# Turned score tiles spilled in woven pairs, with new chunk sizes

## The chip, the cores and the metric

The kernel runs on one core of one Trainium2 chip. The metric is the device time of one execution in microseconds (us). A core has a matrix engine (PE, whose weight loads are PEld), a vector engine (DVE), a scalar engine (ACT), GpSimd (POOL), and SyncE (SP), on whose queue this kernel issues all its DMAs. Each engine works through its own list of instructions in order and waits on semaphores for the others. Sixteen DMA engines carry out what SP issues.

## The reference, cut to what matters

```python
# B=2, S=3136, D=256, d_qk=64, d_ff=1024; everything float32
scores = z @ z.T / S
out    = u * ((np.maximum(scores, 0) ** 2) @ v)          # attention, gated by u
h      = np.maximum(out @ w_in, 0)                       # first MLP
gate   = sigmoid(depthwise_conv3_along_S(h, conv_w))
x      = (h * gate) @ w_out
xn     = (x - mean(x)) / sqrt(var(x) + 1e-6) * g_ln      # second MLP, with layer norm
y      = x + np.maximum(xn @ w_ch1, 0) @ w_ch2
```

## The kernel before, in words

The matrix engine works at reduced precision, so every operand is split in a high part and a remainder, and a product takes three matmuls (high·high, remainder·high, high·remainder).

Attention goes over the queries in chunks. `TILES` gives the chunk sizes of one batch in tiles of 128 tokens (the last tile is half full; 24.5 tiles are one batch); with two batches there are 14 chunks. For chunk `c` and each key tile `j` of 25, two matmuls make the scores in `s` (128 keys x up to 512 queries), ACT takes relu (`a<-s`) and square (`a<-a`; in the first two chunks DVE multiplies a part of them instead), a copy rounds to the high part (`ah<-a`, mostly on ACT), DVE makes the remainder (`al<-a,ah`), and six matmuls add `v` times these into `av`. When a chunk is through, DVE multiplies `av` by `u` (`u<-av,u`), and the result goes to DRAM as `gated`.

The scores are symmetric. So a chunk computes only the key tiles of itself and of later chunks, and those of later chunks are kept: DVE turns each in blocks of 32x32 (`bl<-a`, STREAM_TRANSPOSE), and `spill` writes it to a DRAM tensor `turned`, with four DMAs a tile (one for each band of 32 partitions). A later chunk loads such a tile instead of computing it (`land<-turned`), and goes on with `ah<-land` and `al<-land,ah`. The turned tiles live in four buffers of the tag `bl`, each one tile wide; a buffer is free again when the last DMA out of it has landed. Tiles `a` and `land` share six buffers.

The two MLPs run in 17 blocks of three tiles (the last two of two), each released when its chunks are through: `hps` (first up-projection), the convolution in `t`, `gh` and `gl`, `y` (down-projection), the layer norm, `tps`, `h2ps`, `g2h`, `g2l`, `y`. The last three blocks take their `h` buffers for odd steps from `bl`. Early in the program DVE, ACT and POOL also decode the four weight matrices (`wn`, `wc` and `wih`, `wil` and so on).

The order on each engine is not written by hand. The program is a list of operations with prices, engines and due times (`Program`); a planner walks through it in planned time and lets each engine take the due operation whose inputs and buffers are free. Its plan fixes the order on all five queues. Where it sees a gap on PE, it puts filler matmuls on a tile of zeros (`warm_ps<-zero`, later `y<-zero` or `av<-zero`), which keep PE occupied:

```python
n = int((gaps.get(o, 0.0) - 0.1) / FILL)      # FILL = 0.125 us
```

`LAG0` sets how far behind the attention the first MLP blocks are due. In the planner a spill of `w` columns takes 1.92 us of SP, and lands after 1.9 us plus `w`/300.

Of the kernel before, what the change touches and what calls it, by code (L numbers as in the profile page):

```python
# [8 lines left out]
F32 = mybir.dt.float32  # L9
F32R = mybir.dt.float32r  # L10
U32 = mybir.dt.uint32
AF = mybir.ActivationFunctionType
ALU = mybir.AluOpType
PSUM = bass.MemoryType.PSUM

P = 128
NB, S, D, DQ, DFF = 2, 3136, 256, 64, 1024
# [2 lines left out]
NJ = S // P + 1  # L20
ZW = NJ * P
EPS = 1e-6
TILES = [4, 4, 3, 4, 3, 3, 4]
SQ = 32
PAIR = False
MIRROR = 0
SIZES = [3] * 15 + [2, 2]
WARM = 20
FILL = 0.125
LAG0 = 120.0  # L30
LAG1 = 6.0
LAG2 = 10

# [34 lines left out]
}  # L68

AFTER = {"PE": 0.2, "ACT": 0.165, "DVE": 0.15, "POOL": 0.13, "SP": 0.0}  # L70
RATE, LANDS = 300.0, 1.9
ENGINES = ("PE", "ACT", "DVE", "POOL", "SP")

# [16 lines left out]
class Program:  # L90
# [7 lines left out]
    def op(self, ways, fn, reads=(), writes=(), adds=(), takes=(), due=None, late=None, name="", port=False, kb=None):  # L98


        o = Op()
        o.ways, o.fn, o.due, o.late, o.name, o.port, o.kb = ways, fn, due, late, name, port, kb
        o.before, o.after, o.n = set(), [], len(self.ops)
        o.adds, o.spare = tuple(adds), None
        for k in reads:
            assert k in self.writers, (name, k)
            o.before.update(self.writers[k])
            self.readers.setdefault(k, []).append(o)
        for k in writes:
            o.before.update(self.writers.get(k, ()))  # L110
            o.before.update(self.readers.pop(k, ()))
            self.writers[k] = [o]
        for k in adds:
            o.before.update(self.readers.get(k, ()))
            self.writers.setdefault(k, []).append(o)
        o.before.discard(o)
        bufs = []
        for k in (*reads, *writes, *adds, *((t,) for t in takes)):
            if isinstance(k[0], Buf) and k[0] not in bufs:
                bufs.append(k[0])  # L120
        for b in bufs:
            b.users.append(o)
        o.bufs = bufs
        self.ops.append(o)
        return o

    @staticmethod
    def lasts(o, engine=None, us=None):
        if engine is None:
            engine, us = o.ways[0]  # L130
        return us + (o.late if o.late is not None else AFTER[engine])

# [139 lines left out]
def plan():  # L272
# [5 lines left out]
    for b in range(NB):  # L278
        for i in range(len(TILES)):
            q1 = min(b * S + sum(TILES[: i + 1]) * P, (b + 1) * S)  # L280
            chunks.append((q0, q1))
# [12 lines left out]
def attn_moe_kernel(ctx: ExitStack, tc: tile.TileContext, zt, ut, v, w_in, conv_w, w_out, g_ln, w1, w2, out):  # L294
    nc = tc.nc
    chunks, blocks, after = plan()
    NC, NK = len(chunks), len(blocks)
    CW = max(b - a for a, b in chunks)
# [5 lines left out]
    pool = ctx.enter_context(tc.tile_pool(name="work", bufs=1))  # L304
# [7 lines left out]
    hl = const.tile([P, ZW], F32R, name="hl")  # L312
# [10 lines left out]
    def maker(tag, places, where, shape, dtype):  # L323
# [7 lines left out]
        for tag, places, where, shape, dtype in (  # L331
            ("zst", 1, pool, [P, 512], F32),
            ("st", 2, pool, [P, 1024], F32),
            ("bl", 4, pool, [P, CW], F32),
            ("wc", 1, pool, [P, 512], U32),
            ("wn", 1, pool, [P, 512], U32),
            ("cst", 1, pool, [P, 3 * NF, 2], U32),
# [31 lines left out]
    op = pr.op  # L369
    orders = {}  # L370

    def buf(tag, fixed=False, kind=None):
        if fixed:
            orders[tag] = orders.get(tag, 0) + 1
        return Buf(tag, orders[tag] if fixed else None, kind)

    def at(b, name=None):

        if b.ap is None:
            b.ap = tags[b.tag][1](name or b.tag)  # L380
        return b.ap
# [3 lines left out]
    def price(kind, n):  # L385
        return PRICE[kind](n)
# [16 lines left out]
    def dma(fn, kb, **kw):  # L403
        return op([("SP", 0.45)], lambda e: fn(), late=LANDS + kb / RATE, kb=kb, **kw)
# [5 lines left out]
    def hl_keys(o, n):  # L410
        return [("hl", i, x) for i, (a, b) in enumerate(zp) if a < o + n and o < b for x in "hl"]
# [181 lines left out]
    def half(t, n, a=0, e=None, name=None):  # L593

        return at(t, name)[:, : 2 * n].rearrange("p (k t) -> p k t", k=2)[:, :, a : n if e is None else e]
# [3 lines left out]

    per = len(TILES)  # L600
    start_of = [sum(TILES[:i]) for i in range(per + 1)]
    chunk_of = [i for i, n in enumerate(TILES) for _ in range(n)]

# [9 lines left out]
    turned = {}  # L613
    for c in range(NC):
        i = c % per
        rows = S - start_of[i + 1] * P
        if rows > 0:
            turned[c] = dram.tile([P * TILES[i], rows], F32, tag=f"turned{c}", name="turned")

    def spill(c, j, ab):  # L620
        w = chunks[c][1] - chunks[c][0]
        b = buf("bl")
        op(
            [("DVE", price("dve_turn", w))], lambda e: nc.vector.transpose(at(b, "bl")[:, :w], at(ab)[:, :w]),  # L624
            reads=[(ab, 0)], writes=[(b, 0)], name="bl", port=True,
        )
        k0 = (j - start_of[c % per + 1]) * P

        def write(e):
            blocks_ = at(b)[:, :w].rearrange("p (b k) -> p b k", k=SQ)  # L630
            for o in range(0, min(P, S - j * P), SQ):
                dst = turned[c][:, k0 + o : k0 + o + SQ].rearrange("(b q) k -> q b k", q=SQ)
                nc.sync.dma_start(out=dst, in_=blocks_[o : o + SQ])

        op([("SP", 1.92)], write, reads=[(b, 0)], writes=[("turned", c, j)], late=LANDS + w / RATE, kb=w, due=1e4, name="spill")

    def land(c, j):
        q0, q1 = chunks[c]
        n, i = q1 - q0, chunk_of[j]
        src = c - c % per + i  # L640
        k0 = (start_of[c % per] - start_of[i + 1]) * P
        r0 = (j - start_of[i]) * P
        b = buf("a", True, kind="ld")
        op(
            [("SP", 0.45)],
            lambda e: nc.sync.dma_start(out=at(b, "land")[:, :n], in_=turned[src][r0 : r0 + P, k0 : k0 + n]),
            late=LANDS + n / 2 / RATE, kb=n / 2, writes=[(b, 0)], name="land",
            reads=[("turned", src, jj) for jj in range(start_of[c % per], start_of[c % per + 1])],
        )
        return b  # L650

    def scores(c, j, due):
        q0, q1 = chunks[c]
        n = q1 - q0
        from_dram = mirrored(c, j)
        ab = land(c, j) if from_dram else buf("a", True)

        def a():
            return at(ab, "a")[:, :n]

        if not from_dram:
            products(c, j, ab, a, due)
# [5 lines left out]
        if spilled(c, j):  # L668
            spill(c, j, ab)
# [16 lines left out]
    def products(c, j, ab, a, due):  # L686
        q0, q1 = chunks[c]
        n, o = q1 - q0, q0 % S
        ps, lh = buf("w", kind="s"), lh_b[c]

        def mm(e):
            p = at(ps, "s")[:, :n]
            zj = hl[:, j * P : (j + 1) * P]
            nc.tensor.matmul(p, zj, hl[:, o : o + n], start=True, stop=False)  # L694
            nc.tensor.matmul(p, zj, at(lh)[:, :n], start=False, stop=True)  # L695

        lh_keys = [(lh, 0)] if c == 0 else [(lh, 0), (lh, 1)]
        op(
            [("PE", 2 * price("mm", n))], mm, reads=sorted({*hl_keys(j * P, P), *hl_keys(o, n)}) + lh_keys,
            writes=[(ps, 0)], takes=[ab], due=due, name=f"s{c}.{j}",  # L700
        )
        op(
            [("ACT", price("act_ps", n))], lambda e: nc.scalar.activation(a(), at(ps)[:, :n], AF.Relu),  # L703
            reads=[(ps, 0)], writes=[(ab, 0)], name="relu",
        )
        if c < FUSED[0] and j % FUSED[1] < FUSED[2]:
            op(
                [("DVE", price("dve_ps", n))], lambda e: nc.vector.tensor_tensor(a(), a(), at(ps)[:, :n], ALU.mult),  # L708
                reads=[(ps, 0)], writes=[(ab, 0)], name="square",
            )  # L710
        else:
            op([("ACT", price("act", n))], lambda e: nc.scalar.activation(a(), a(), AF.Square), writes=[(ab, 0)], name="square")  # L712
# [10 lines left out]
    def sums(b):  # L723
        return at(b, "av").rearrange("p a b -> p (a b)").rearrange("p (d q) -> p d q", d=2)
# [22 lines left out]
    def gate_u(c):  # L747
        q0, q1 = chunks[c]
        n = q1 - q0
        u, b = u_b[c], av_b[c]  # L750
        for d in range(2):
            op(
                [("DVE", price("dve_ps", n))],
                lambda e, d=d: nc.vector.scalar_tensor_tensor(
                    half(u, n)[:, d, :], sums(b)[:, d, :n], 1.0 / S**2, half(u, n)[:, d, :], ALU.mult, ALU.mult
                ),
                reads=[(b, d)], writes=[(u, d)], name="gate_x",
            )
        dma(
            lambda: nc.sync.dma_start(out=gated[:, :, q0 + 1 : q1 + 1], in_=half(u, n)),  # L760
            n, reads=[(u, 0), (u, 1)], writes=[("gated", c)], name="x out",
        )
# [321 lines left out]
    for c in range(NC):  # L1084
# [14 lines left out]
        for i in (i for i in range(NK) if after[i] == c):  # L1099
            length = (blocks[i][1] - blocks[i][0]) / NT * begin[NC]  # L1100
            pace = max(pace, begin[max(c + 1, 2) if PAIR else c + 1])
            if c >= NC - 2:
                length = LENGTH[i - NK]
            lag = max(LAG1, LAG0 * (1 - c / LAG2))
            when[i] = lambda x, pace=pace, lag=lag, length=length: 2 * (pace + lag + x * length)
# [32 lines left out]
    for o in order:  # L1138
# [8 lines left out]
        n = int((gaps.get(o, 0.0) - 0.1) / FILL)  # L1147
# [5 lines left out]
    for i in list(nc.cur_bb.bb.instructions):  # L1153
        e = str(i.engine)
# [47 lines left out]
```

## Time and profile before

| what | value |
|---|---|
| median of 3 runs | 1125.02 us (1124.41 to 1125.16) |
| the profiled execution | 1121.42 us |
| its span, from the first to the last instruction | 1119.3 us |
| PE busy | 1098.5 us, 98% of the span |
| DVE, ACT busy | 857.9 us (77%), 714.5 us (64%) |
| granted PE clock | 1.00 in all stretches but the last |
| DMA issues of spills (`turned<-bl`) | 372 of 64 KB, 188 of 48 KB |

The span is what the engines' rows cover; the 2.1 us around it belong to the execution's start and end. Busy time of PE is the union of overlapping matmuls whose ends are modelled, so 98% does not mean that PE works at its peak rate: one 512-column matmul is shown as about 0.4 us, while the next one starts 0.23 us after it.

### The profile page before, as it was taken

The page shows a single profiled execution, that of the slowest core. Times are in us where ns is not written, and L with a number is a line of the kernel's source. Part 1 is how long each engine was busy: PE and PEld are TensorE (multiplying, and loading weights), DVE is VectorE, ACT ScalarE, POOL GpSimd, SP SyncE. Part 2 cuts the span into 40 slices and gives each one's busy share as a digit, 9 for nine tenths or more (in the row PEclk, how much of TensorE's full clock was granted, in tenths as well). Part 3 has the DMA queues.
Part 4 walks back from the last instruction along what each step waited for, and adds up shares of the span by engine and source line. Part 5 has one row for each costly group of instructions (what it writes and reads, how often), then busy time and mean ns, then how long its engine had stood idle before and what let it go on. Part 6 is the DMA issues. An engine that isn't in the chain of part 4 may idle for free.

```text
span 1119.3 us, 18987 instructions
## 1 busy us (share of the span) xinstructions
PE 1098.5 (98%) x6686; PEld 1028.0 (92%) x6686; DVE 857.9 (77%) x1810; ACT 714.5 (64%) x1473; POOL 30.4 (3%) x43
## 2 busy tenths in 40 slices
PE   9899999999999999999999999999999999999998
PEld 7777787899999989999999999999999999999998
DVE  7888889989869686868687778785857868477773
ACT  7668767786647576757665666664737647366552
POOL 2000000000000000000000000000000000000000
PEclk9999999999999999999999999999999999999999
DMA  7788877975444224253316242412433524220000
GB/s 199 149 199 157 198 148 181 225 179 175 96 126 134 76 64 81 43 90 83 70 44 109 83 78 63 103 50 51 90 109 92 146 65 122 76 82 27 25 15 19
DMA packets 327054, 115.41 MB, mean 103 GB/s; under 512 B 276528, under 2 KB 314800, under 8 KB 326960
## 3 DMA queue, kind: packets, MB, share of 16 engines
q1 hardware_dynamic: 326960, 114.21, 42.2%
q8 instruction: 52, 0.85, 0.3%
q14 instruction: 42, 0.34, 0.1%
HBM read 64.74 MB, written 46.47 MB: 99 GB/s over the span
## 4 chain that ended last, share of the span: by engine, by line
PE 85%; DVE 4%; DMA 4%; ACT 4%; issue 1%; SPq 1%; POOL 0%; DVEq 0%; ACTq 0%
PE av L739 10%; PE av L736 10%; PE av L738 10%; PE y L839 8%; PE y L837 8%; PE y L838 8%; PE h2ps L821 4%; PE h2ps L822 4%; PE h2ps L823 4%; PE hps L821 4%; PE hps L822 4%; PE hps L823 4%; PE s L694 3%; PE s L695 3%; DMA land<-turned 2%; DVE al L673 2%
## 5 line engine op out<-in xcount | busy, mean ns | idle before, releaser
L736 PE MATMUL av<-ah,vh 128*128 128x512 f32 (+2 forms) x700 | 258.5, 369 | 5.1 <-ACT ah L393 2.3
L739 PE MATMUL av<-ah,vl 128*128 128x512 f32 (+2 forms) x700 | 256.0, 366 | 0.0
L738 PE MATMUL av<-al,vh 128*128 128x384 f32 (+2 forms) x672 | 248.3, 370 | 6.6 <-DVE al L673 6.1
L1015 DVE SCALAR_TENSOR_TENSOR g2l<-h2ps,g2h 128x384 fp32r<-128x384 f32 (+1 forms) x136 | 73.2, 539 | 125.1 <-ACT g2h L1010 124.4
L1010 ACT ACTIVATE g2h<-h2ps 128x384 fp32r<-128x384 f32 (+1 forms) x136 | 65.1, 479 | 146.2 <-PE h2ps L823 145.5
L736 PEld LDWEIGHTS av<-ah,vh 128*128 128x128 f32 x700 | 131.7, 188 | 19.8 <-ACT ah L393 5.0
L738 PEld LDWEIGHTS av<-al,vh 128*128 128x128 f32 x672 | 126.4, 188 | 23.2 <-DVE al L673 13.2
L739 PEld LDWEIGHTS av<-ah,vl 128*128 128x128 f32 x700 | 131.6, 188 | 14.1
L703 ACT ACTIVATE a<-s 128x512 f32<-128x512 f32 (+2 forms) x196 | 105.9, 558 | 45.5 <-PE s L695 45.1
L673 DVE TENSOR_TENSOR al<-a,ah 128x512 fp32r<-128x512 f32 (+2 forms) x182 | 114.2, 637 | 9.2 <-ACT ah L393 8.5
L837 PE MATMUL y<-woh,gh 128*128 128x256 f32 x392 | 109.7, 280 | 0.7 <-DVE ysb L1023 0.7
L839 PE MATMUL y<-woh,gl 128*128 128x256 f32 x392 | 109.9, 280 | 0.3 <-DVE gl L903 0.3
L837 PE MATMUL y<-w2h,g2h 128*128 128x256 f32 x392 | 109.8, 280 | 0.2 <-DVE ysb L1023 0.2
L624 DVE STREAM_TRANSPOSE bl<-a 128x512 f32<-128x512 f32 (+1 forms) x146 | 95.0, 657 | 19.4 <-ACT a L712 9.9
L839 PE MATMUL y<-w2h,g2l 128*128 128x256 f32 x392 | 109.8, 280 | 0.0
L838 PE MATMUL y<-w2l,g2h 128*128 128x256 f32 x392 | 109.7, 280 | 0.0
L838 PE MATMUL y<-wol,gh 128*128 128x256 f32 x392 | 109.6, 280 | 0.0
L393 ACT CAST ah<-a 128x512 fp32r<-128x512 f32 (+2 forms) x185 | 105.8, 583 | 4.4 <-DVE a L708 3.2
L712 ACT ACTIVATE a<-a 128x512 f32<-128x512 f32 (+2 forms) x183 | 105.9, 593 | 1.4
L673 DVE TENSOR_TENSOR al<-land,ah 128x384 fp32r<-128x384 f32 (+2 forms) x154 | 90.3, 595 | 16.5 <-ACT ah L393 15.8
L863 ACT ACTIVATE t<-h,cw 128x384 f32<-128x384 f32 (+1 forms) x136 | 81.9, 605 | 27.8 <-DVE gl L903 26.6
L393 ACT CAST ah<-land 128x384 fp32r<-128x384 f32 (+2 forms) x146 | 78.5, 547 | 31.5 <-DMA land<-turned 22.4
(119 smaller groups left out, 2442.9 us busy)
## 6 DMA issues: line engine op xcount, KB each, us to landing
turned<-bl SPq DMA_DIRECT2D x372, 64.0 KB, 1.9
land<-turned SPq DMA_DIRECT2D x82, 192.0 KB, 3.1
land<-turned SPq DMA_DIRECT2D x42, 224.0 KB, 3.9
turned<-bl SPq DMA_DIRECT2D x188, 48.0 KB, 1.8
land<-turned SPq DMA_DIRECT2D x30, 256.0 KB, 3.4
out_dram<-ysb SPq DMA_DIRECT2D x15, 384.0 KB, 2.8
vst<-in_v_dram SPq DMA_DIRECT2D x11, 512.0 KB, 4.0
x<-gated SPq DMA_DIRECT2D x14, 386.0 KB, 3.8
```

Of the source, the lines that this page charges most:

```text
L393: nc.scalar.copy(dst, src)
L624: [("DVE", price("dve_turn", w))], lambda e: nc.vector.transpose(at(b, "bl")[:, :w], at(ab)[:, :w]),
L673: lambda e: nc.vector.tensor_tensor(at(al, "al")[:, :n], a(), f(at(ah)[:, :n]), ALU.subtract),
L703: [("ACT", price("act_ps", n))], lambda e: nc.scalar.activation(a(), at(ps)[:, :n], AF.Relu),
L712: op([("ACT", price("act", n))], lambda e: nc.scalar.activation(a(), a(), AF.Square), writes=[(ab, 0)], name="square")
L736: nc.tensor.matmul(p, vhj, at(ah)[:, :n], start=first(b, d), stop=False, **kw)
L738: nc.tensor.matmul(p, vhj, at(al)[:, :n], start=False, stop=False, **kw)
L739: nc.tensor.matmul(p, vlj, at(ah)[:, :n], start=False, stop=False, **kw)
L821: nc.tensor.matmul(p, a, h_, start=d == 0, stop=False)
L837: nc.tensor.matmul(p, a, wh, start=first(acc, (i0 + i) // 2), stop=False, **kw)
L838: nc.tensor.matmul(p, a, wl, start=False, stop=False, **kw)
L839: nc.tensor.matmul(p, b, wh, start=False, stop=k == NF - 1, **kw)
```

## The change

Two turned tiles with neighbouring `j` now go into one buffer. The two transposes write their 32-column blocks in turn (block of the first tile, block of the second, and so on), and four DMAs write both tiles, in runs of 256 bytes instead of 128. The tag `bl` has two buffers of two tiles instead of four of one. For this, in a woven chunk (all but the first and the last of a batch) the queries stand in a changed order: for each 32-token part `o`, the part of every tile `j` in turn. The score matmuls read `hl` and `lh` in that order, `land` picks its rows by it, and the multiplication by `u` puts the tokens back. Tiles that belong to a batch's last chunk stay single, in runs of 128 bytes, and take a whole buffer. The factor 1/S moves from the gate into relu and square. Chunk sizes, `LAG0` and the planner's prices for spills change, and with them the planned order on all engines.

```diff
-TILES = [4, 4, 3, 4, 3, 3, 4]
+TILES = [4, 4, 4, 4, 4, 2, 3]
-LAG0 = 120.0
+LAG0 = 100.0
+ISSUE, SHORT = 0.62, {1: 1.1, 2: 1.5}
-            ("bl", 4, pool, [P, CW], F32),
+            ("bl", 2, pool, [P, 2 * CW], F32),
+    def woven(c):
+        i = c % per
+        return TILES[i] if 0 < i < per - 1 else 0
+    def weave(t, c):
+        k = woven(c)
+        return t.rearrange("p (j o s) -> p o j s", j=k, s=SQ) if k else t
+    def unweave(t, c):
+        k = woven(c)
+        return t.rearrange("p (o j s) -> p j o s", j=k, s=SQ) if k else t
     def spill(c, j, ab):
         w = chunks[c][1] - chunks[c][0]
-        b = buf("bl")
-        op(
-            [("DVE", price("dve_turn", w))], lambda e: nc.vector.transpose(at(b, "bl")[:, :w], at(ab)[:, :w]),
-            reads=[(ab, 0)], writes=[(b, 0)], name="bl", port=True,
-        )
+        to = chunk_of[j]
+        k, a = woven(c - c % per + to), j - start_of[to]
+        m = min(2, k - a + a % 2) if k else 1
+        b = held.pop((c, j), None)
+        if b is None:
+            b = buf("bl")
+            if m == 2:
+                held[c, j + 1] = b
+        def turn(e):
+            t = at(b, "bl")[:, : m * w].rearrange("p (b m s) -> p b m s", m=m, s=SQ)[:, :, a % m, :]
+            nc.vector.transpose(t, at(ab)[:, :w].rearrange("p (b s) -> p b s", s=SQ))
+        op([("DVE", price("dve_turn", w))], turn, reads=[(ab, 0)], writes=[(b, a % m)], name="bl", port=True)
+        if a % m < m - 1:
+            return
         def write(e):
-            blocks_ = at(b)[:, :w].rearrange("p (b k) -> p b k", k=SQ)
-            for o in range(0, min(P, S - j * P), SQ):
-                dst = turned[c][:, k0 + o : k0 + o + SQ].rearrange("(b q) k -> q b k", q=SQ)
-                nc.sync.dma_start(out=dst, in_=blocks_[o : o + SQ])
+            blocks_ = at(b)[:, : m * w].rearrange("p (b k) -> p b k", k=m * SQ)
+            for o in range(min(P, S - j * P) // SQ):
+                at_ = k0 + ((o * k + a0) if k else (a * P // SQ + o)) * SQ
+                dst = turned[c][:, at_ : at_ + m * SQ].rearrange("(b q) k -> q b k", q=SQ)
+                nc.sync.dma_start(out=dst, in_=blocks_[o * SQ : (o + 1) * SQ])
-        op([("SP", 1.92)], write, reads=[(b, 0)], writes=[("turned", c, j)], late=LANDS + w / RATE, kb=w, due=1e4, name="spill")
+        op(
+            [("SP", 4 * ISSUE)], write, reads=[(b, x) for x in range(m)],
+            writes=[("turned", c, x) for x in range(j - m + 1, j + 1)],
+            late=LANDS + SHORT[m] * w / RATE, kb=SHORT[m] * w, due=1e4, name="spill",
+        )
-            nc.tensor.matmul(p, zj, hl[:, o : o + n], start=True, stop=False)
-            nc.tensor.matmul(p, zj, at(lh)[:, :n], start=False, stop=True)
+            nc.tensor.matmul(p, zj, weave(hl[:, o : o + n], c), start=True, stop=False)
+            nc.tensor.matmul(p, zj, weave(at(lh)[:, :n], c), start=False, stop=True)
-            [("ACT", price("act_ps", n))], lambda e: nc.scalar.activation(a(), at(ps)[:, :n], AF.Relu),
+            [("ACT", price("act_ps", n))], lambda e: nc.scalar.activation(a(), at(ps)[:, :n], AF.Relu, scale=1.0 / S),
-                lambda e, d=d: nc.vector.scalar_tensor_tensor(
-                    half(u, n)[:, d, :], sums(b)[:, d, :n], 1.0 / S**2, half(u, n)[:, d, :], ALU.mult, ALU.mult
+                lambda e, d=d: nc.vector.tensor_tensor(
+                    natural(half(u, n)[:, d, :], c), unweave(sums(b)[:, d, :n], c), natural(half(u, n)[:, d, :], c), ALU.mult
```

How the order changes is seen best at three places. The first is SP's queue in the first chunk, from where the first turned tiles leave. Names with a number are buffers or tensors; `zst`, `vst` and `wst` are loads of z, v and weights. Before:

```order
L417 DMA zst_287<-in_zt_dram 128x512
L633 DMA turned_82<-bl_277 32x16x32 x4
L633 DMA turned_82<-bl_300 32x16x32 x4
L633 DMA turned_82<-bl_314 32x16x32 x4
L417 DMA zst_389<-in_zt_dram 128x512
L633 DMA turned_82<-bl_385 32x16x32 x4
L633 DMA turned_82<-bl_411 32x16x32 x4
L633 DMA turned_82<-bl_429 32x16x32 x4
```

And now:

```order
L419 DMA zst_287<-in_zt_dram 128x512
L672 DMA turned_82<-bl_277 32x16x64 x4
L419 DMA zst_379<-in_zt_dram 128x512
L672 DMA turned_82<-bl_313 32x16x64 x4
L672 DMA turned_82<-bl_401 32x16x64 x4
L419 DMA zst_445<-in_zt_dram 128x512
L455 DMA vst_454<-in_v_dram 128x2x256
L465 DMA vst_454<-in_v_dram 64x256 x2
L544 DMA wst_476<-in_w_in_dram 128x1024
```

The same six tiles leave with 12 issues in place of 24, and the loads behind them stand nearer. In the whole program the spills' issues fall from 560 to 320, of which 300 have 16 blocks (some in runs of 256 bytes, some of 128) and 20 have 8.

The second place is DVE's list at the same point: from the second transpose of the first pair to the transpose that takes the same buffer again (`bl_401`, the third buffer in a tag of two). It stands so in the changed kernel:

```order
L659 STREAM_TRANSPOSE bl_277<-a_269 128x16x32
L507 TENSOR_SCALAR wc_229<-wc_229 128x24
L725 TENSOR_TENSOR al_302<-a_269,ah_294 128x512
L659 STREAM_TRANSPOSE bl_313<-a_292 128x16x32
L508 TENSOR_SCALAR wc_229<-wc_229 128x24
L760 SCALAR_TENSOR_TENSOR a_326<-s_279,a_326 128x512
L725 TENSOR_TENSOR al_352<-a_292,ah_315 128x512
...
L427 TENSOR_TENSOR hl_70<-zst_287,hl_70 64x512
L659 STREAM_TRANSPOSE bl_313<-a_311 128x16x32
L725 TENSOR_TENSOR al_386<-a_354,ah_371 128x512
L725 TENSOR_TENSOR al_396<-a_356,ah_377 128x512
L659 STREAM_TRANSPOSE bl_401<-a_326 128x16x32
```

Before, the rows there are the same in kind and order, but each transpose had a buffer of its own, and the fifth (`bl_411`) took the first one's again; the two rows left out are `al` rows as the others.

The third place is PE's list near the end, in the last three MLP blocks, where filler stands between the down-projections `y`. Before:

```order
L839 MATMUL y_12977<-woh_75,gl_12975 128x256
L1128 MATMUL y_12977<-zero_99 128x256 x30
L837 MATMUL y_12977<-woh_75,gh_13037 128x256
...
L839 MATMUL y_12977<-woh_75,gl_13051 128x256
L1128 MATMUL y_12977<-zero_99 128x256 x4
L837 MATMUL y_12977<-woh_75,gh_13061 128x256
```

And now:

```order
L890 MATMUL y_12656<-wol_76,gh_12613 128x256
L891 MATMUL y_12656<-woh_75,gl_12619 128x256
L1180 MATMUL y_12656<-zero_99 128x256 x17
L889 MATMUL y_12656<-woh_75,gh_12725 128x256
L890 MATMUL y_12656<-wol_76,gh_12725 128x256
```

There are 17 fillers in one piece where there were 34 in two; 24 of the block's `y` matmuls now stand ahead of them instead of 12.

## Rows read from the trace of the kernel before

**Rows 1.** Busy time by stretch, with instruction counts, granted clock, DMA share and GB/s.

```profile
0.00:66.00 66.00, 59.37 (x270) 47.92 (x271) 52.82 (x93) 46.06 (x88) 9.23 (x19) 1.00 0.77 171
66.00:120.00 54.00, 51.26 (x231) 40.63 (x230) 46.75 (x84) 41.92 (x82) 0.74 (x2) 1.00 0.84 177
120.00:165.00 45.00, 42.73 (x235) 38.77 (x234) 38.18 (x80) 34.28 (x78) 1.26 (x2) 1.00 0.83 179
165.00:214.00 49.00, 47.57 (x224) 38.96 (x223) 44.96 (x87) 36.53 (x71) 0.63 (x1) 1.00 0.79 184
214.00:262.00 48.00, 46.90 (x282) 45.29 (x281) 43.42 (x100) 34.59 (x75) 0.88 (x1) 1.00 0.68 178
...
400.00:1048.00 648.00, 646.50 (x4050) 616.36 (x4049) 477.14 (x1019) 402.51 (x823) 11.49 (x12) 1.00 0.33 79
```

**Rows 2.** PE's instructions by shape, 0 to 262 us: first and last of 25 rows.

```profile
L736 PE MATMUL av<-ah,vh 128*128 128x512 f32 x150 | 59.7, 398 | 3.3 <-DVE ah L679 1.6 <-ACT ah L393 1.5 <-DVE u L754 0.2
...
L982 PE MATMUL tps<-ident,xn 128*128 128x128 f32 x6 | 0.8, 272 | 0.0
```

**Rows 3.** Timeline of PE, 814 to 816 us: start, duration, instruction.

```profile
814.00 0.39 PE L736 MATMUL av<-ah,vh 128*128 128x512 f32 x1
...
815.39 0.40 PE L739 MATMUL av<-ah,vl 128*128 128x512 f32 x1
815.63 0.34 PE L694 MATMUL s<-hl 128*128 128x384 f32 x1
```

**Rows 4.** Chain that ended last, by line, 0 to 262 us.

```profile
by line: PE av L738 10.0%; PE av L739 9.9%; PE av L736 9.4%; DMA land<-turned 8.2%; DVE al L673 6.5%; DMA turned<-bl 5.9%; issue 5.6%; ACT ah L393 4.8%; SPq L633 4.6%; ACT a L703 3.8%; ACT a L712 3.6%; DVE bl L624 3.0%; PE s L695 2.3%; PE s
```

**Rows 5.** Timeline of SP: DMA issues in unbroken pieces.

```profile
35.94 12.42 SPq L633 DMA_DIRECT2D turned<-bl  x20
...
97.30 13.13 SPq L633 DMA_DIRECT2D turned<-bl  x24
```

**Rows 6.** Spills' issues between 19 and 165 us (durations in ns).

```profile
L633 SPq DMA_DIRECT2D turned<-bl x200: 302/490/1785, 18.8 to 163.9; - x100
```

**Rows 7.** What SP waited for, 19 to 165 us: longest of 22 rows.

```profile
SPq L633 <- DVE al L673: 2.9, 8, 0.5
```

**Rows 8.** What SP waited for, 165 to 262 us: longest of 26 rows.

```profile
SPq L589 <- DMA gated<-u: 7.2, 2, 4.8
```

**Rows 9.** Who waited for whom, 0 to 262 us: total, times, longest.

```profile
ACT ah L393 <- DMA land<-turned: 17.4, 12, 3.2
...
DVE bl L624 <- DMA turned<-bl: 6.3, 5, 2.6
```

**Rows 10.** The page on DMA packets and queues, and issues with median us to landing.

```profile
DMA packets 327054, 115.41 MB, mean 103 GB/s; under 512 B 276528, under 2 KB 314800, under 8 KB 326960
...
q1 hardware_dynamic: 326960, 114.21, 42.2%
...
turned<-bl SPq DMA_DIRECT2D x372, 64.0 KB, 1.9
...
lh<-hl SPq DMA_DIRECT2D x10, 128.0 KB, 2.5
```

**Rows 11.** Busy time after the last spill.

```profile
945.00:1048.00 103.00, 102.32 (x667) 99.44 (x666) 72.11 (x156) 57.68 (x117) 0.95 (x2) 1.00 0.22 68
```

**Rows 12.** Timeline of DVE, 36 to 39 us.

```profile
37.28 1.25 DVE L673 TENSOR_TENSOR al<-a,ah 128x512 fp32r<-128x512 f32 x2
```

**Rows 13.** DVE's instructions by shape: strided reads (`wn`), plain ones (`wc`).

```profile
L513 DVE TENSOR_SCALAR wn<-wst 128x512 uint32<-128x512 uint32 x16 | 6.7, 420 | 1.2 <-DMA wst<-in_w_in_dram 1.2
L506 DVE TENSOR_SCALAR wc<-wc 128x512 uint32<-128x512 uint32 x16 | 6.7, 418 | 0.0
```

**Rows 14.** Timeline of PE, 1048 to 1070 us.

```profile
1052.92 3.75 PE L1128 MATMUL y<-zero 128*128 128x256 f32 x30
1056.50 0.28 PE L837 MATMUL y<-woh,gh 128*128 128x256 f32 x1
...
1056.94 0.38 PE L839 MATMUL y<-woh,gl 128*128 128x256 f32 x1
```

More of the change, by code (lines that the diff above doesn't have):

```diff
@@ L618, in attn_moe_kernel, with natural @@
             turned[c] = dram.tile([P * TILES[i], rows], F32, tag=f"turned{c}", name="turned")
+    def woven(c):
[7 more added lines that the diff above has]
+        return t.rearrange("p (o j s) -> p j o s", j=k, s=SQ) if k else t
+    def natural(t, c):
+        k = woven(c)
+        return t.rearrange("p (j o s) -> p j o s", j=k, s=SQ) if k else t
@@ L620, in spill @@
+    held = {}
     def spill(c, j, ab):
         w = chunks[c][1] - chunks[c][0]
-        b = buf("bl")
-        op(
-            [("DVE", price("dve_turn", w))], lambda e: nc.vector.transpose(at(b, "bl")[:, :w], at(ab)[:, :w]),
-            reads=[(ab, 0)], writes=[(b, 0)], name="bl", port=True,
-        )
-        k0 = (j - start_of[c % per + 1]) * P
-        def write(e):
-            blocks_ = at(b)[:, :w].rearrange("p (b k) -> p b k", k=SQ)
-            for o in range(0, min(P, S - j * P), SQ):
-                dst = turned[c][:, k0 + o : k0 + o + SQ].rearrange("(b q) k -> q b k", q=SQ)
-                nc.sync.dma_start(out=dst, in_=blocks_[o : o + SQ])
@@ new lines, in spill, with write @@
+        op([("DVE", price("dve_turn", w))], turn, reads=[(ab, 0)], writes=[(b, a % m)], name="bl", port=True)
+        if a % m < m - 1:
+            return
+        k0 = (start_of[to] - start_of[c % per + 1]) * P
+        a0 = a - m + 1
+        def write(e):
+            blocks_ = at(b)[:, : m * w].rearrange("p (b k) -> p b k", k=m * SQ)
[3 more added lines that the diff above has]
+                nc.sync.dma_start(out=dst, in_=blocks_[o * SQ : (o + 1) * SQ])
@@ L643, in land, with read @@
         b = buf("a", True, kind="ld")
+        def read(e):
+            src_ = turned[src][:, k0 : k0 + n]
+            if woven(src):
+                src_ = src_.rearrange("(o j q) k -> j o q k", j=woven(src), q=SQ)[j - start_of[i]]
+            else:
+                src_ = src_[r0 : r0 + P]
+            nc.sync.dma_start(out=at(b, "land")[:, :n], in_=src_)
         op(
             [("SP", 0.45)],
-            lambda e: nc.sync.dma_start(out=at(b, "land")[:, :n], in_=turned[src][r0 : r0 + P, k0 : k0 + n]),
+            read,
             late=LANDS + n / 2 / RATE, kb=n / 2, writes=[(b, 0)], name="land",
@@ L707, in products @@
             op(
-                [("DVE", price("dve_ps", n))], lambda e: nc.vector.tensor_tensor(a(), a(), at(ps)[:, :n], ALU.mult),
+                [("DVE", price("dve_ps", n))], lambda e: nc.vector.scalar_tensor_tensor(a(), at(ps)[:, :n], 1.0 / S, a(), ALU.mult, ALU.mult),
                 reads=[(ps, 0)], writes=[(ab, 0)], name="square",
```

## The prediction

> **What bounds the kernel now.** I read the busy times by stretch first. PE's granted clock is 1.00 throughout. From 400 to 1048 us PE is busy 646.5 of 648 us, while up to 262 us it shows gaps in every stretch [rows 1]. Its busy time overlaps, so I count work instead. At the steady rate six 512-column matmuls start within 1.39 us, 0.232 us each, and two of 384 columns start 0.17 us apart, the same per column [rows 3]. The 25 rows by shape for 0 to 262 us [rows 2] add up to 564 matmuls of 512 columns, 350 of 384 for the attention, 106 of 384 and 386 for the MLPs, 108 of 256, six turns and 99 fillers. Priced per column (256 columns from the filler, 30 between 1052.92 and 1056.50, 0.119 us each [rows 14]) that is 130.8 + 60.9 + 18.5 + 12.9 + about 0.7 = 224 us of work and 11.8 of filler. So PE loses 262 - 236 = 26 us in this stretch. About 4 of them belong to the start, before v has arrived; 22 are stalls that the plan did not foresee. Everything that the change can win on PE lies there and in the filler.
>
> Next the chain that ended last. In the first 262 us it runs for 4.6% through the issuing of spills on SP (L633), 5.9% through spills under way and 8.2% through loads of turned tiles [rows 4]: 12.1 + 15.5 + 21.5 = 49 us. The rest alternates between DVE, ACT and PE. A chain has others close beside it, so 49 us isn't the price of the spills; it says where to look.
>
> On SP's own timeline 20 spill issues stand in 12.42 us and 24 in 13.13 us with nothing between [rows 5]: 0.62 and 0.55 us each, 0.58 on the average, though one alone takes a median of 0.49 [rows 6]. There are 200 between 19 and 165 us: 116 of 146 us. SP waits only 14.9 us in that time (22 rows, longest 2.9) [rows 7], against 41.7 us in the 97 us from 165 on (26 rows) [rows 8]. A 512-column tile needs 4 x 0.58 = 2.3 us of SP, and on PE eight matmuls, 8 x 0.232 = 1.86 us. So up to 165 us SP's queue is full, and everything behind it is late: DVE stands 6.3 us for a spill buffer, ACT 17.4 us for loaded tiles [rows 9].
>
> **SP's issues.** Pairs cut the issues. In the changed kernel's first three chunks, of four tiles each, 21, 17 and 13 tiles are spilled. Three of each are single (4 + 4 + 2 issues, the last tile being half); the others make 9, 7 and 5 pairs of four issues: 46 + 38 + 30 = 114 for 200. If one still costs 0.58 us, SP has 66 us of spills instead of 116. The price could follow the bytes behind an issue, then nothing is saved; but the 64 KB and the 48 KB issues both have hundreds of runs of 128 bytes, a pair's issue has as many runs as a 64 KB one, and the alone price is 0.49 whatever waits behind. I take 0.58. SP then has some 60 us to spare in 146 and stops setting the pace.
>
> What this gives is limited by the next in line, DVE. Its busy share was 0.80, 0.866 and 0.848 up to 165 us, and 0.918 and 0.905 afterwards, where SP had room [rows 1]. The weights are decoded on both sides of that mark, so I take 0.91 as what DVE reaches when SP doesn't hold it. The stretch to 120 then ends 54 - 46.75/0.91 = 2.6 us sooner, the next 45 - 38.18/0.91 = 3.0 us; of the first stretch, where the start lowers the share, I take 3 us, two thirds of the waits for buffers, most of which lie there. After 165 us shorter landings may give half a microsecond. Together 9 us. Bounds: nothing, if other waits hold DVE; and 16 us, if the whole 226 us of DVE work up to 262 us went at the best share (226.1/0.918 = 246).
>
> **The DMA engines.** 560 spill issues have 372 x 512 + 188 x 384 = 262,656 runs of 128 bytes, nearly all of the 276,528 packets under 512 bytes; the queue takes 42.2% of 16 engines [rows 10], 7,557 us. After the last spill 68 GB/s need a share of 0.22 [rows 11], 0.052 ns a byte. At that rate the other 80.6 MB need 4,190 us, which leaves 12.8 ns a run of 128 bytes, of which 6.7 are bytes and 6.1 are fixed. A run of 256 would take 19.4 against 25.6 for two. From 19 to 165 us the 200 issues of some 480 runs take 1,230 us of 146 x 16, a share of 0.5 of the 0.77 to 0.84 there [rows 1]; with most of them in pairs the whole falls by about 0.1. This is the half microsecond above and a part of the 9.
>
> [...] The rows here have no 256-byte run to judge by.
>
> **DVE's and ACT's work.** The transposes write 32-column blocks 64 columns apart. No row shows a strided write; a read of every second word takes 420 ns where a plain one takes 418 [rows 13], so I take nothing. The same number of queries is spilled in 10 tiles fewer (136 for 146), which is under 2 us of DVE over the program. Relu with a scale, and the multiplications with the constant moved, keep their operands: nothing.
>
> **PE's work.** Attention keeps its count of matmuls; per column wide and narrow cost the same, so nothing changes. The scores fall from 196 to 186 tiles but cover 715 units of 128 columns instead of 712: 3 x 2 matmuls x 0.058 = 0.35 us more. Reading the queries in runs of 32 columns: no row on PE shows it; nothing by the strided reads of DVE, and see the rivals.
>
> **Filler.** Up to the place in the order where PE has done 224 us of work, the changed list has 118 fillers for 99: 19 x 0.119 = 2.3 us at most, nothing where PE would have waited anyway. I take 1 us lost. Near the end 17 stand for 34, 2.0 us; but before, the remainder `gl` came 0.2 us after the 30 fillers were through [rows 14], so they covered a real wait. With 12 more matmuls ahead of it, it should have shrunk: 1.5 us won, between 0 and 2.
>
> **Sum.** -9 + 1 - 1.5 + 0.3 = -9.2. The profiled execution, 1121.4 us (span 1119.3 and 2.1 around it), would become 1112.2. The median is 3.6 above that execution, so I predict 1115.8.
>
> **The rivals.** *No change.* What keeps DVE at 0.85 is the handing to and fro with ACT (`ah`, then `al`), not the queue; then chunks two and three need the same share, the 9 us are 0, and the sum is +1 - 1.5 + 0.3: 1125. For it speaks that the waits for buffers are only 6.3 us [rows 9], against it that the share rises just where SP gets room.
>
> *Slower: two buffers are too few.* A pair's buffer can be taken again after four issues (2.3 us) and the last landing: 1.9 us for a 64 KB spill, 2.5 for 128 KB within the chip [rows 10]: 4.2 to 4.8 us. In the order's piece DVE has ten large and two small instructions until then; two large ones take 1.25 us [rows 12], so some 6.5 us. It decides when landing takes more than 4.2 us. Some 25 of the reuses in the first four chunks are that close. At a landing of 5 us each costs 0.8, 20 us, of which DVE's idle tenth of 262 us takes perhaps half; the 9 us of SP stay half: about +5, 1130. The singles at a chunk's end, of which only two can be under way, push the same way. Also on this side: PE reads the woven queries more slowly. That concerns 240 score matmuls of 512 columns and 20 of 256, 58 us; at a rate a quarter lower +14, less the 9: 1130.
>
> *The end gives more.* DVE and SP keep step, and all of the 16 us come: 1108.
>
> **How the numbers follow.** The forecast with the fuller gain beside it gets 0.72 (the latter 0.15 of it), no change 0.14, two buffers 0.10, slow reading 0.04. From no change a measurement tells about 0.2%, 2.2 us. Faster is then 0.72, same 0.14, slower 0.14. The forecast's own range is 1105 to 1121; to leave out no more than 2 in 10, with no change inside and the slower cases up to their middle, it becomes 1104 to 1128.
>
> **What would show it.** Right: some 114 spill issues in the first three chunks at 0.5 to 0.6 us, SP waiting for tens of microseconds there; no wait of DVE for spills under way; shorter waits for landed tiles; DVE's share near 0.91 by 165 us; DMA share near 0.72; score matmuls starting 0.23 us apart; everything after 300 us about 8 us earlier and in the same step, with 1 to 2 us less at the end. Wrong: issues at over 1 us, `bl` waiting for its DMAs at each second pair, transposes over 0.75 us, or matmuls on woven queries farther apart. If all the steps hold and PE still stalls before 262 us, DVE and ACT were the bound.

## The result, and the profile after

The changed kernel takes 1131.81 us (1129.91 to 1134.13, four runs), the kernel before beside it 1124.72 us (1122.72 to 1125.16, four runs). The ratio is 1.0067 [1.0045, 1.009]: slower by 0.7%, where 0.8% faster was forecast. The profiled execution took 1132.36 us, its span 1130.6.

Up to 165 us the trace looks much as it was forecast; after that it doesn't. The busy times by stretch, after the change (columns as in [rows 1]):

```profile
0.00:66.00 66.00, 63.94 (x302) 52.91 (x303) 59.01 (x107) 50.10 (x97) 6.60 (x16) 1.00 0.74 199
66.00:120.00 54.00, 52.26 (x246) 42.85 (x245) 49.91 (x90) 41.99 (x82) 3.06 (x3) 1.00 0.72 179
120.00:165.00 45.00, 44.89 (x212) 37.49 (x213) 43.42 (x84) 37.12 (x74) 0.00 (x0) 1.00 0.64 176
165.00:214.00 49.00, 43.59 (x196) 34.56 (x195) 38.31 (x79) 32.80 (x63) 2.43 (x3) 0.97 0.58 171
214.00:262.00 48.00, 46.33 (x259) 40.92 (x258) 41.93 (x82) 30.56 (x59) 1.24 (x2) 1.00 0.57 159
262.00:312.00 50.00, 47.66 (x262) 41.92 (x262) 36.64 (x76) 28.71 (x59) 0.87 (x1) 0.97 0.42 115
400.00:1048.00 648.00, 640.98 (x3943) 593.44 (x3943) 477.29 (x1006) 406.63 (x819) 9.92 (x11) 1.00 0.29 80
```

In the first three stretches PE is busy 161.1 us instead of 153.4, DVE 152.3 instead of 137.8 [rows 1], and the DMA share is lower. From 165 to 214 us it turns round: PE 43.59 us where it had 47.57, at a granted clock of 0.97.

SP's spill issues from 19 to 165 us, the transposes there, and two of the 24 rows of what SP's queue waited for (us in total, times, longest):

```profile
L672 SPq DMA_DIRECT2D turned<-bl x109: 302/488/2252, 20.0 to 164.8; - x109
L659 DVE STREAM_TRANSPOSE bl<-a x49: 661/703/712, 19.3 to 163.3; 128x512 f32<-128x512 f32 x49
```

```profile
SPq L672 <- DVE bl L659: 35.8, 14, 5.7
...
SPq L544 <- DVE bl L659: 0.2, 1, 0.2
```

The 24 rows add up to 65.4 us, where [rows 7] had 14.9: SP's queue is no longer full. No engine waits for a buffer of `bl`.

The chain that ended last, of the first 262 us (start us, us, what). Before it had 8.2% in loads of turned tiles [rows 4]; these are the longest of the 17.8% that it has now:

```profile
161.59 6.79 DMA land<-turned
...
185.59 10.04 DMA land<-turned
...
199.91 7.16 DMA land<-turned
...
236.41 6.63 DMA land<-turned
...
244.70 12.81 DMA land<-turned
```

And the waits for loaded tiles over the whole span:

```profile
ACT ah L395 <- DMA land<-turned: 51.9, 45, 3.8
...
DVE ah L399 <- DMA land<-turned: 7.4, 6, 3.6
```

Together that is 59.3 us. Before, it was 22.7 us over the whole span (ACT 22.4, DVE 0.3). In the first 262 us alone the totals hardly differ (17.4 us before [rows 9], 15.5 now), so the totals do not tell what PE loses.

One such load in detail. SP issues it at 199.91 us. DVE is through with all else at 203.56 and stands until it has landed; PE has its last matmul before that at 203.10. SP, DVE and PE on the timeline (start us, us, engine, line, operation, operands, idle before):

```profile
199.91 0.53 SPq L694 DMA_DIRECT2D land<-turned  x1
...
207.17 0.43 DVE L399 CAST ah<-land 128x512 fp32r<-128x512 f32 x1 [3.62 <-DMA land<-turned]
...
207.85 0.68 DVE L725 TENSOR_TENSOR al<-land,ah 128x512 fp32r<-128x512 f32 x1
...
203.10 0.40 PE L747 MATMUL s<-lh,hl 128*128 128x512 f32 x1
207.65 0.79 PE L788 MATMUL av<-ah,vh 128*128 128x512 f32 x1 [4.16 <-DVE ah L399]
208.59 0.79 PE L790 MATMUL av<-al,vh 128*128 128x512 f32 x1
209.18 0.63 PE L791 MATMUL av<-ah,vl 128*128 128x512 f32 x1
209.61 0.63 PE L788 MATMUL av<-ah,vh 128*128 128x512 f32 x1
...
211.17 0.40 PE L747 MATMUL s<-lh,hl 128*128 128x512 f32 x1
```

PE stands idle 4.16 us. Afterwards its matmuls start 0.94, 0.59 and 0.43 us apart, and are back at 0.23 by 211.17 us: the seven steps from 207.65 us on take 3.5 us instead of 1.6. The first of them is no matter of the clock, since the second matmul needs DVE's `al`, which is through only at 208.53 us. The other six take 2.6 us instead of 1.4, and the granted clock of these stretches says why: it was 0.50 from 208 to 211 us.

```profile
201.00:205.00 4.00, 2.49 (x11) 1.59 (x9) 2.56 (x5) 1.64 (x3) 0.00 (x0) 1.00 0.43 101
205.00:209.00 4.00, 1.21 (x2) 0.70 (x3) 1.83 (x4) 0.00 (x0) 0.00 (x0) 0.82 0.45 143
208.00:209.00 1.00, 0.86 (x2) 0.41 (x2) 1.00 (x2) 0.00 (x0) 0.00 (x0) 0.50 0.27 104
209.00:214.00 5.00, 5.00 (x21) 4.24 (x21) 3.52 (x11) 4.21 (x8) 0.00 (x0) 0.80 0.26 102
```

### The profile page after: what moved, and what is told of

Read it like the earlier page. It is cut to its first block, busy times and chain, and to the rows that moved or that the text cites. A ratio compares the mean times of both kernels' runs of the same rounds, so it can differ in the third digit from the quotient of the medians.

```text
span 1130.6 us, 18602 instructions
## 1 busy us (share of the span) xinstructions
PE 1104.1 (98%) x6670; PEld 1007.1 (89%) x6670; DVE 861.9 (76%) x1803; ACT 714.6 (63%) x1449; POOL 29.6 (3%) x44
## 4 chain that ended last, share of the span: by engine, by line
PE 71%; DMA 13%; DVE 7%; ACT 5%; issue 2%; SPq 1%; DVEq 0%; POOL 0%; ACTq 0%
DMA land<-turned 12%; PE av L788 8%; PE av L791 8%; PE av L790 8%; PE y L891 7%; PE y L889 7%; PE y L890 7%; PE h2ps L874 4%; PE h2ps L873 4%; PE h2ps L875 4%; PE hps L873 3%; PE hps L874 3%; PE hps L875 3%; PE s L746 2%; PE s L747 2%
## 5 line engine op out<-in xcount | busy, mean ns | idle before, releaser
L790 PE MATMUL av<-al,vh 128*128 128x512 f32 (+2 forms) x672 | 248.9, 370 | 2.9 <-DVE al L725 2.3
L725 DVE TENSOR_TENSOR al<-land,ah 128x512 fp32r<-128x512 f32 (+2 forms) x164 | 92.2, 570 | 48.0 <-ACT ah L395 46.8
L395 ACT CAST ah<-land 128x512 fp32r<-128x512 f32 (+2 forms) x153 | 78.9, 525 | 72.3 <-DMA land<-turned 51.9
L659 DVE STREAM_TRANSPOSE bl<-a 128x512 f32<-128x512 f32 (+1 forms) x136 | 92.7, 690 | 10.4 <-ACT a L764 9.7
L924 DVE SCALAR_TENSOR_TENSOR t<-h,cw,t 128x384 f32<-128x384 f32 (+1 forms) x136 | 80.6, 595 | 17.1 <-ACT t L915 17.0
```

The costliest lines, as they stand in the source:

```text
L395: nc.scalar.copy(dst, src)
L659: nc.vector.transpose(t, at(ab)[:, :w].rearrange("p (b s) -> p b s", s=SQ))
L725: lambda e: nc.vector.tensor_tensor(at(al, "al")[:, :n], a(), f(at(ah)[:, :n]), ALU.subtract),
L790: nc.tensor.matmul(p, vhj, at(al)[:, :n], start=False, stop=False, **kw)
L924: lambda e, h=h, t=t, k=k: nc.vector.scalar_tensor_tensor(at(t)[:, :n], at(h)[:, 1 : 1 + n], cw[:, k, 1:2], at(t)[:, :n], ALU.mult, ALU.add),
```

## The experiments

**The theories.** A: the woven `land` is what costs. Its source counts the four 32-row parts first, then the rows of a part, and by this theory only four of the sixteen DMA engines carry it out, so that it lands late: with woven loads alone under way the DMA share was 0.27 from 208 to 209 us and 0.26 from 209 to 214 (the last rows above), where four of sixteen would be 0.25. The rival, B: the loads are no dearer than before, and the new sizes and due times, which move the calls for tiles, make them late. C: the weaving itself costs, on DVE or PE. (D and E come with a later expectation.) Two runs split or undo the load's shape, one puts that shape into the kernel before, and four take sizes, lag and pairs apart.

**Each woven load in four DMAs.** One for each part, so that no DMA counts parts first; 348 issues more.

```diff
             if woven(src):
                 src_ = src_.rearrange("(o j q) k -> j o q k", j=woven(src), q=SQ)[j - start_of[i]]
+                for o in range(4):
+                    nc.sync.dma_start(out=at(b, "land")[o * SQ : (o + 1) * SQ, :n], in_=src_[o])
...
```

> The changed kernel with each load of a woven tile issued as four DMAs of 32 rows; order and buffers are the same. Theory A (the one woven load is carried out by 4 of the 16 DMA engines, because its source counts 4 parts first, and lands in 6 to 13 us): the loads land in 3 to 5 us again, the 52 us that ACT waits for them fall under 20, the clock stays at 1.00, and the time is 1108 to 1118 us, below the kernel before. Theory B (chunk sizes and plan ask for the loads too late and too densely): the waits stay and the time is 1128 to 1138, more with 348 issues added on SP. Theory C (weaving costs on DVE or PE): unchanged, 1128 to 1134.

Measured: 1126.63 us (1125.62 to 1128.75), ratio 1.0040 [1.0026, 1.0054]; only a little better than the change itself, and outside every range that was expected. The issues of the woven tiles on SP, and their KB and median time from issue to landing:

```profile
L693 SPq DMA_DIRECT2D land<-turned x464: 302/419/1547, 137.2 to 1007.9; - x155
```

```profile
land<-turned SPq DMA_DIRECT2D x192, 64.0 KB, 2.2
```

Each quarter of a 256 KB tile lands 2.2 us after its issue, but a tile needs four issues, and waits for loaded tiles are still 34.9 us on ACT. SP's share of the chain rises from 1 to 3%. By its total the run doesn't decide: it takes A's cost away and puts 348 issues of about 0.42 us, some 146 us of SP, in its place. But the two stand at different times. Up to 312 us PE is as busy as with the plain loads further down, to the digit:

```profile
165.00:214.00 49.00, 48.47 (x233) 40.11 (x232) 44.75 (x91) 38.33 (x72) 3.06 (x4) 1.00 0.64 176
...
262.00:312.00 50.00, 50.00 (x309) 45.95 (x309) 34.00 (x73) 25.90 (x54) 0.87 (x1) 1.00 0.41 105
```

From 165 to 312 us ACT and DVE wait 1.1 us for loaded tiles, where the changed kernel has 22.5. The loss comes after that: from 312 to 420 us, where the quarters' issues are 12.4% of the chain that ended last and the loads 15.6%, and again after 800 us.

**The load's shape alone, in the kernel before.** The rows of `turned` get one unused row after each 32, in the chunks that the change weaves; nothing else differs. A load then counts four groups first; 106 do so (the 154 loads less the 48 from the first chunks of the batches).

```diff
-            turned[c] = dram.tile([P * TILES[i], rows], F32, tag=f"turned{c}", name="turned")
+            turned[c] = dram.tile([4 * (SQ + padded(c)) * TILES[i], rows], F32, tag=f"turned{c}", name="turned")
...
-                dst = turned[c][:, k0 + o : k0 + o + SQ].rearrange("(b q) k -> q b k", q=SQ)
+                dst = turned[c][:, k0 + o : k0 + o + SQ].rearrange("(b q) k -> q b k", q=SQ + padded(c))[:SQ]
...
+                src_ = src_.rearrange("(b q) k -> b q k", q=SQ + 1)[r0 // SQ : r0 // SQ + 4, :SQ]
```

> The kernel before, with the spilled rows in groups of 32 set apart by one unused row, so that the loads from the middle chunks' tiles count 4 parts first, as in the changed kernel; nothing is woven, order and sizes are the same. Theory A: 106 loads run on 4 engines each, 1272 four-byte packets fewer, and the time rises by 8 to 25 us, to 1133 to 1150. Theories B and C: no change, 1122 to 1127.

Measured: 1184.7 us (1183.35 to 1186.15), ratio 1.0554 [1.0538, 1.0569]. The direction is A's, the size far over what A expected (1133 to 1150). The waits for loaded tiles and the stretches from 120 to 214 us:

```profile
ACT ah L393 <- DMA land<-turned: 109.0, 69, 5.4
```

```profile
120.00:165.00 45.00, 39.58 (x210) 36.53 (x208) 33.92 (x71) 29.18 (x66) 0.64 (x1) 0.96 0.75 165
165.00:214.00 49.00, 41.78 (x180) 34.06 (x181) 36.87 (x70) 30.57 (x59) 1.24 (x2) 0.93 0.59 143
```

Sizes, lag, order, and number and size of the spills are those of before, so the rival can't have made this; nor can rows that lie far apart, since here only one row is skipped.

**Sizes and lag alone, on the kernel before.**

```diff
-TILES = [4, 4, 3, 4, 3, 3, 4]
+TILES = [4, 4, 4, 4, 4, 2, 3]
-LAG0 = 120.0
+LAG0 = 100.0
```

> The kernel before with the new chunk sizes and the new lag alone. Theory A: the sizes do not matter much, 1119 to 1130. Theory B: they are what costs, 1130 to 1140. Theory C: as A.

Measured: 1112.95 us (1112.52 to 1113.79), ratio 0.9915 [0.990, 0.993]; waits for loaded tiles 12.3 us. On the kernel before, these numbers don't cost anything: they win 10 us, more than either side thought. For the changed kernel the next run tells.

**The change with the old sizes and lag.** The same two lines, back from new to old.

> The changed kernel with the old chunk sizes and the old lag. Theory A: the woven loads are slow here too, 1126 to 1140. Theory B: the loss is gone and the weaving shows its gain, 1110 to 1120. Theory C: 1128 to 1136.

Measured: 1154.7 us (1152.57 to 1157.56), ratio 1.0288 [1.0267, 1.0309]; ACT waits 68.4 us for loaded tiles; that is slower than any theory expected. So the sizes and the lag don't hurt the change, they soften it, and the rival falls.

**The change with plain loads.** The transposes put the 32-column blocks where they belong by token, so that `turned` has its rows in natural order and a load takes 128 rows that follow one another. Pairs, runs of 256 bytes, woven queries, sizes and the order on every engine stay; only these access patterns differ.

```diff
-            t = at(b, "bl")[:, : m * w].rearrange("p (b m s) -> p b m s", m=m, s=SQ)[:, :, a % m, :]
-            nc.vector.transpose(t, at(ab)[:, :w].rearrange("p (b s) -> p b s", s=SQ))
+            q = woven(c) or 1
+            t = at(b, "bl")[:, : m * w].rearrange("p (j o m s) -> p o j m s", j=q, m=m, s=SQ)[:, :, :, a % m, :]
+            nc.vector.transpose(t, at(ab)[:, :w].rearrange("p (o j s) -> p o j s", j=q, s=SQ))
...
-            nc.sync.dma_start(out=at(b, "land")[:, :n], in_=src_)
+            nc.sync.dma_start(out=at(b, "land")[:, :n], in_=src_[r0 : r0 + P])
```

> The changed kernel, with the transposes of a woven chunk writing their 32-column blocks in the natural order of tiles, so that a tile's 128 rows stand together in DRAM and are loaded by one plain DMA over all 16 engines; sizes, buffers, order and issues as changed. Theory A (slow loads were the whole loss, and pairs free SP and DVE as forecast): ACT waits under 15 us for loads, 1100 to 1110 us, below the 1113 of the new sizes alone. Theory D (slow loads were the loss, but pairs give nothing that the new sizes alone do not): 1110 to 1116. Theory E (two buffers, or the plan made with the new spill prices, cost as well): 1117 to 1128.

Measured: 1105.86 us (1105.65 to 1106.08), ratio 0.9856 [0.984, 0.9872]: it beats both kernels, the changed one by 26 us (24 by the ratios), and lies in A's range. The woven queries and the interleaved transposes are still there, so C does not explain the loss. The chain, the only wait that is still put down to a load, and three stretches:

```profile
PE 92%; ACT 2%; DVE 2%; DMA 2%; issue 1%; SPq 0%; POOL 0%; DVEq 0%
```

```profile
ACT a L752 <- DMA land<-turned: 4.0, 1, 4.0
```

```profile
165.00:214.00 49.00, 48.47 (x234) 40.43 (x234) 45.07 (x93) 37.75 (x72) 3.05 (x4) 1.00 0.60 175
214.00:262.00 48.00, 48.00 (x281) 43.55 (x280) 43.61 (x85) 33.06 (x63) 0.62 (x1) 1.00 0.61 180
262.00:312.00 50.00, 50.00 (x310) 45.95 (x309) 33.98 (x73) 25.78 (x54) 0.86 (x1) 1.00 0.41 108
```

In the detail above the load came late for two reasons. With plain loads it lands 3.0 us after its issue, not 7.16; and it is issued at 193.69 us, not at 199.91, because the eight spill issues ahead of it on SP's queue, right behind three loads, take 5.12 us (here the changed kernel, then plain loads):

```profile
189.20 10.62 SPq L672 DMA_DIRECT2D turned<-bl  x8
```

```profile
188.47 5.12 SPq L673 DMA_DIRECT2D turned<-bl  x8
```

So behind woven loads SP's own issuing is slower as well: 1.33 us for an issue here, against 0.64. What holds it was not traced.

PE has the same 6,670 instructions in the same order in this kernel and the changed one, so the fillers are landmarks: the same filler in both shows how far the changed kernel is behind. After the change:

```profile
167.88 0.28 PE L1180 MATMUL y<-zero 128*128 128x256 f32 x1
...
234.88 0.28 PE L1180 MATMUL y<-zero 128*128 128x256 f32 x1
...
361.77 0.28 PE L1180 MATMUL av<-zero 128*128 128x256 f32 x1
...
1067.73 2.19 PE L1180 MATMUL y<-zero 128*128 128x256 f32 x17
```

And with plain loads:

```profile
167.81 0.40 PE L1177 MATMUL y<-zero 128*128 128x256 f32 x2
...
227.11 0.28 PE L1177 MATMUL y<-zero 128*128 128x256 f32 x1
...
345.43 0.28 PE L1177 MATMUL av<-zero 128*128 128x256 f32 x1
...
1041.26 2.19 PE L1177 MATMUL y<-zero 128*128 128x256 f32 x17
```

The lag is 0.07, 7.8, 16.3 and 26.5 us. Matched in the same way, instruction by instruction, it is 9.9 us at 262 us and 20.3 us at 450 us, stays there until 900, and grows to 26.5 by 1050. So the loss begins with the woven loads and pauses when the first batch's are through. The second batch's start at about 671 us, but up to 900 us PE falls no further behind (ACT waits 7.1 us for loads between 420 and 900 us); after that the loss comes back, smaller.

The packet counts say what differs in the transfers. The pages' DMA lines of the changed kernel, of plain loads, and of the padded kernel:

```profile
DMA packets 219324, 114.98 MB, mean 102 GB/s; under 512 B 167520, under 2 KB 198112, under 8 KB 219232
```

```profile
DMA packets 220716, 114.98 MB, mean 104 GB/s; under 512 B 168912, under 2 KB 199504, under 8 KB 220624
```

```profile
DMA packets 325782, 115.40 MB, mean 98 GB/s; under 512 B 275256, under 2 KB 313528, under 8 KB 325688
```

With the same bytes the changed kernel has 1,392 small packets fewer than the one with plain loads: 116 woven loads (464 quarters above) times 12. The padded kernel has 1,272 fewer than the kernel before [rows 10]: 106 loads times 12. In the traces of the kernel before and of the changed one they can be counted by size, 4 bytes: the queue of the first has 13,616 of them, 16 for each of its 851 DMAs; that of the second has 8,544, as 16 for each of 505 DMAs and 4 for each of the 116 woven loads make. That fits theory A, if an engine that takes part writes one such packet; that it does is the author's reading, since the trace names no engine. The quarter-load run agrees too: its queue has 6,960 packets more than the changed kernel's, 116 loads times 60 (four DMAs with 16 small packets each in place of one with four). In the trace's semaphore updates a woven load has five in place of sixteen (1,276 fewer in all, 116 times 11): one about 1 us after its issue, and four that end with its landing. Counted off so, the 48 woven loads of 256 KB land a median of 7.3 us after their issue; the 80 of that size in the kernel with plain loads have 3.6.

**The same with the old sizes and lag.**

> The same with the old chunk sizes and the old lag: pairs alone against the kernel before, without the slow loads. Theory A: 1108 to 1117. Theory D: 1120 to 1125. Theory E: 1126 to 1136; the 4-engine loads then cost the rest of the 32 us that the old sizes with woven loads lost.

Measured: 1113.14 us (1111.95 to 1114.67), ratio 0.9922 [0.9906, 0.9938], waits for loaded tiles 2.1 us; in A's range. Without the slow loads the rest of the change (pairs, and the plan that was made with them) wins 9.0 us. Against the change with old sizes the woven load costs 1154.7 - 1113.1 = 41.6 us here.

**The new sizes with the old lag, on the kernel before.** Only the line of `TILES` changes.

> The kernel before with the new chunk sizes and the old lag of 120: tells whether sizes or lag gave the 10 us. Sizes: 1110 to 1116. Lag: 1119 to 1127.

Measured: 1118.49 us, ratio 0.9965 [0.9951, 0.9979] (median of five, one of them 2177 us long and left out of the ratio); between the two ranges expected. Sizes alone win about 4 us, the shorter lag another 5.5.

## Why the prediction was wrong, step by step

**The step that failed** is in "What this gives": "After 165 us shorter landings may give half a microsecond", and with it "shorter waits for landed tiles" among the signs. The diff said that `land` picks its rows in the woven order, and the working gave this read no term, neither a price nor a bound, and no rival had it. In its place the runs showed loads on four engines, which land late (a share of 0.26 to 0.27 of the sixteen, a median of 7.3 us for 256 KB, against 3.6) and slow SP's issues behind them (1.33 us each in the piece above, against 0.64). An estimate could have been had from rows: 68 GB/s at a share of 0.22 [rows 11] are 19 GB/s an engine, so 256 KB take 0.85 us on sixteen and 3.4 us on four, and more where those four have spills queued too. Beside a plain 256 KB load's median of 3.6 us (the quarter-load run has 32 such) that makes at least 6, and the chain shows 6.6 to 12.8. What that costs depends on the slack: 26 us in the changed kernel, 42 with the old sizes, 62 in the kernel before. That SP's full queue leaves least slack there is argued, not shown.

Of the 26.5 us by which the spans differ, PE's idle time takes 15.5 (26.5 against 11.0, span less busy), the other 11.0 are longer busy time. The granted clock, 0.996 against 1.000 over the span, accounts for about 4.5 of that by estimate; the remaining 6.5 are not resolved, since the ends of matmuls are modelled.

**SP's issues** were right: 109 spill issues by 165 us (forecast 114), a median of 488 ns, and 65 us of waiting where 60 were forecast to spare. (The 0.49 us that the prediction calls the price of an issue alone is the median of all 200 [rows 6], those of the full queue among them.) After 165 us, behind woven loads, the price did not hold: 1.33 us an issue in the piece shown above.

**DVE as the next limit** was right: its share was 0.89, 0.92 and 0.96 up to 165 us (0.91 was taken), and PE got 7.7 us more busy time by then, where 8.6 were forecast; 12 fillers more (103 for 91), some 1.4 us, are in it. **Nine microseconds for the pairs** agree with the old sizes and plain loads (9.0), and are 7.1 with the new sizes (1112.95 to 1105.86). That they agree so closely is luck in part: the runs compare whole kernels, the end and the filler included (with old sizes and pairs 152 fillers stand up to 165 us, where before had 91), and no run shows the nine by themselves.

**The DMA engines**: the share was 0.74, 0.72 and 0.64 in place of 0.77, 0.84 and 0.83 [rows 1]; about 0.72 was forecast. The GB/s are about the same, so the longer runs do save engine time: in the trace a packet of 128 bytes takes a mean of 12 ns of an engine and one of 256 bytes 16, where 12.8 and 19.4 were worked out. **DVE's strided writes** cost nothing: a transpose has a median of 703 ns before and after, and in the best kernel, with its blocks farther apart, 704. **PE's woven reading** has no rate a quarter lower: at 211 us, behind the detail above, score matmuls on woven queries start at 211.17, 211.40, 211.64 and the next matmul at 211.88, 0.23 to 0.24 us apart.

**The filler**: 118 up to 262 us, as forecast (103 on `warm_ps` and 15 on `y`); what they cost there no run shows. At the end 17 stand for 2.03 us (1041.26 to 1043.29) where 30 took 3.58 [rows 14] and four more 0.47: 2.0 us won, of 1.5 forecast. It is no gain of the pairs: with the new sizes and lag alone the same 17 stand there (at 1048.24 us).

**Sizes and lag** were taken as neutral but for 0.3 us of score columns and the filler. They win 10 us on the kernel before [0.990, 0.993], the gain at the end among them, and 7.3 with pairs and plain loads (1113.14 to 1105.86). So with plain loads, too, the forecast of 1115.8 would have been 10 us off, on the other side. Part of what the shorter lag wins is filler: from 400 to 1048 us the old lag leaves 33 of them, the new one 2, which is 3.7 us at 0.119 each if PE would not have waited instead; the rest was not traced.

**The rivals.** "Two buffers are too few" is dead: nobody waits for `bl` in the changed kernel or with plain loads, and with the old sizes DVE does so once, for 0.3 and 0.6 us. "No change" is dead too: with plain loads the pairs win. "PE reads the woven queries more slowly" does not show (its price was worked out too low: at a rate a quarter lower, 58 us become 77, 19 more and not 14). "The end gives more" named 1108, and plain loads reach 1105.9, though 7 of those 16 us come from sizes and lag. The slower side that came true was none of those listed.

**Still open**: how far SP's 348 more issues explain the loss of the quarter loads after 312 us (the chain names them, no run takes them away), why SP's issues take longer behind woven loads, and how the price goes with other numbers of groups, which wasn't tried.

## What to carry to other kernels

When a change reorders data in DRAM, cost every reader of it, not only the writer it was made for: look at which dimension a load's access pattern counts first, and how many parts that has (four here, with a median of 7.3 us until 256 KB had landed, against 3.6 for plain loads). If a side that costs nothing can absorb the permutation (here the transposes' output pattern), put it there and leave both DMAs plain; that turned a loss of 7 us into a gain of 16. A count of small packets that is short by a fixed number for each DMA (12 here) shows the fault in the profile without another run.

## What the runs showed of the hardware that was not expected

A load whose source counted four groups first had exactly 12 small packets fewer (1,392 over 116 loads, 1,272 over 106), and one unused row after each 32 was enough for that: it made a tuned kernel 5.5% slower. Eight spill issues behind three such loads took SP 10.62 us, and 5.12 behind plain ones. At the end of a gap of 4.16 us on PE the granted clock fell to 0.50 (208 to 211 us), and six matmuls' steps there took 2.6 us instead of 1.4. A STREAM_TRANSPOSE into blocks spread over a buffer twice as wide took a median of 703 to 704 ns, as the plain one before did.
